# Windowed attention and a sine feed-forward on one core: crossbar transposes for batches 4 to 7, and a reordered start

## The chip, the cores and the metric

The kernel runs on one core of a Trainium2 chip. The metric is the device time in microseconds (us) of the whole program, the median of several runs. TensorE (PE in the profile) does matrix products, VectorE (DVE) and ScalarE (ACT) elementwise work, GpSimd (POOL) elementwise work and most loads, and SyncE (SP) issues copies and stores. In the profile's names KS and QS hold K and Q, VW the two layouts of V, VgX the rows of V of the global positions, and osb a tile of the output.

## The reference, cut to what matters

```python
# 8 batches, 8 heads, 576 positions, 64 per head; 8 global positions
scores = scale * q @ k^T
mask = |i - j| <= 32  or  i is global  or  j is global
attn = softmax(where(mask, scores, -1e9))
x = (attn @ v) as 4608 tokens x 512
h = x @ w_in                      # 512 x 2048
g = h + sin(alpha * h)**2 / (alpha + 1e-9)
out = g @ w_out                   # 2048 x 512
```

## The kernel before

The 4608 tokens are nine chunks of 512, and a batch is 576 tokens. Stage b (b = 1 to 7) is the attention of batch b, woven with the second matmul (`@ w_out`) of chunk b-1, and then the first matmul (`@ w_in`) of chunk b. A stage's length is measured here from the start of one first matmul to the start of the next (the first `hb<-xT` row of each chunk in the trace), so the length given for stage 1 holds the first matmul of chunk 0 and the attention of batch 1, and so on.

K and Q come in with positions on partitions, and TensorE transposes them for a pair of heads at a time. In stage b it transposes those of batch b+1:

```python
def T_half(src, b, hp, out):
    for jt in range(NTW):                       # 6 slices of 96 positions
        for t, pr in heads:
            nc.tensor.transpose(out=out[pr, jt*TW:(jt+1)*TW],
                in_=src[:, 2*hp + t, jt, :], identity=identb[0:TW, 0:TW])
# T_K, T_Q: T_half into PSUM, then one copy to kTw (VectorE) or qT (ScalarE)
```

V of a batch is used in two layouts. The second is made by SyncE with two DMAs inside SBUF once V has landed, and two more DMAs write the rows of the global positions:

```python
def shift_v(b, eng=nc.sync):
    eng.dma_start(out=W[0:64, 1], in_=W[QB:QB+64, 0])           # 384 KB
    eng.dma_start(out=W[64:KB, 1, :, 0:(NU-1)*D], in_=...)      # 240 KB
def global_v(b): ...                                             # 2 x 48 KB, SyncE
```

`gather_kq` loads the rows of K and Q of the global positions. The order of a stage's pieces is a list `parts` (one step of the attention each), into which the groups of the second matmul (`fill`, by `counts`) and loads are chained:

```python
counts = [1, 1, 1, 1, 1, 1, 2, 2, 4]
if p + 1 < B:
    with_extra(parts, load_slots(p + 1), 0, 4)   # K, Q in halves, then V: batch p+1
    if p < 3:
        parts[4] = partial(chain, parts[4], partial(gather_kq, p + 1))
    for hp in range(NHP):                        # global columns of K, Q (GpSimd)
        parts[hp + LEAD + 1] = partial(chain, ..., partial(globals_in, p + 1, hp))
...
if p == 0:
    m1[5] = partial(chain, m1[5], *vs)           # shift_v(1), global_v(1)
    m1[6] = partial(chain, m1[6], w_loads[3])    # second half of w_out
```

At the end of each attention, VectorE computes the 8 global columns (`xg`) and GpSimd inserts them into `xT` (8 copies). The first matmul waits for these insertions.

The softmax here doesn't subtract the row's maximum and nothing guards it: scores larger than these inputs give would overflow.

## Time and profile before

| | before |
|---|---|
| median of 3 runs | 361.02 us (360.83 to 362.65) |
| span of the profiled run | 356.8 us, granted clock 1.0 |
| PE busy | 336.7 us (94%) |
| stages 1 to 7, us | 40.19, 39.64, 36.94, 38.04, 36.71, 36.73, 34.42 |

The stage lengths are differences of starts in the instructions in order of time. The chain of work that ended last, by engine, from the page of before:

```profile
PE 65%; ACT 13%; DMA 7%; POOL 6%; issue 4%; DVE 3%; POOLq 1%; ACTq 0%; DVEq 0%
```

Two thirds of the chain is TensorE's own work (PEq, POOLq and the like are an engine's sequencer). SyncE's DMA issues in order of time (start, duration, queue, line, operation, out<-in, count), before:

```profile
37.85 0.57 SPq L143 DMA_DIRECT2D VW<-VW  x1
...
39.30 1.36 SPq L152 DMA_DIRECT2D VW<-VgX  x2
64.90 11.43 SPq L715 DMA_DIRECT2D out_dram<-osb  x4
```

The shifted copies of V of batch 1 are issued at 37.85, some 22 us before their first use at 60.21 and 27 us before SyncE's first output store.

### The profile page before, as it was taken

To read this page: it belongs to the slowest core of one execution; us is meant where nothing else is said; L and a number is where in the kernel's file an instruction comes from. 1 tells how busy PE (TensorE), PEld (TensorE's weight loads), DVE (VectorE), ACT (ScalarE), POOL (GpSimd) and SP (SyncE) were. 2 spreads that over 40 slices of the span, in tenths; PEclk is the share of its full clock that TensorE was granted. 3 is DMA by queue.
4 is the path that set the end of the run, shared out by engine and by line. 5 is a ranking of instruction groups with operands and counts; after the bars stand their busy time and mean duration, and the time that the engine had idled before them with its cause. 6 is when DMAs were issued, how large, how long until landed. Compare 5 with 4: busy or idle time off the path is not lost.

```text
span 356.8 us, 9407 instructions
## 1 busy us (share of the span) xinstructions
PE 336.7 (94%) x3738; PEld 172.0 (48%) x3738; DVE 237.4 (67%) x527; ACT 245.9 (69%) x376; POOL 205.6 (58%) x302
## 2 busy tenths in 40 slices
PE   6686997999999999999989999999999999999996
PEld 5563444444455445544554446444544444444444
DVE  5765784758775687668764878487848764875610
ACT  3756885847894889578975888488848884844401
POOL 9858897355871787169805791579247205755000
PEclk9999999999999999999999999999999999999999
DMA  9999999940598429940995099409931001001012
GB/s 75 166 196 184 199 170 179 182 136 20 35 171 104 112 17 168 122 114 3 165 115 134 2 121 154 136 8 90 181 105 43 30 32 61 0 2 59 31 59 88
DMA packets 133149, 35.39 MB, mean 99 GB/s; under 512 B 121794, under 2 KB 126818, under 8 KB 133106
## 3 DMA queue, kind: packets, MB, share of 16 engines
q0 software_dynamic: 123120, 20.04, 77.5%
q1 hardware_dynamic: 9682, 14.63, 13.9%
q8 instruction: 29, 0.48, 0.5%
q10 hardware_dynamic: 304, 0.14, 0.1%
q14 instruction: 14, 0.11, 0.1%
HBM read 38.95 MB, written 9.44 MB: 136 GB/s over the span
## 4 chain that ended last, share of the span: by engine, by line
PE 65%; ACT 13%; DMA 7%; POOL 6%; issue 4%; DVE 3%; POOLq 1%; ACTq 0%; DVEq 0%
PE hb L664 28%; PE o L703 12%; PE ops L703 12%; DMA w_out<-in_moe_w_out_dram 4%; ACT E L507 3%; PE num L553 3%; PE Sp L501 2%; DVE H2b L654 2%; ACT L607 2%; PE den L535 2%; DMA QS<-in_q_dram 2%; PE hb L703 2%; ACT Sb L671 2%; ACT lnd L541 2%; ACT L614 2%
## 5 line engine op out<-in xcount | busy, mean ns | idle before, releaser
L671 ACT ACTIVATE Sb<-hb,alphaT 128x512 bf16<-128x512 f32 x144 | 96.9, 684 | 57.6 <-PE hb L664 54.2
L664 PE MATMUL hb<-xT,w_in 128*128 128x512 bf16 x576 | 128.9, 379 | 1.6 <-POOL xT L588 1.4
L681 POOL TENSOR_TENSOR S<-Sb 128x512 bf16<-128x512 bf16 x94 | 96.0, 1041 | 48.2 <-ACT Sb L671 44.8
L654 DVE SCALAR_TENSOR_TENSOR H2b<-S,recipT,hb 128x512 bf16<-128x512 bf16 x144 | 102.4, 740 | 30.7 <-POOL S L681 30.3
L664 PEld LDWEIGHTS <-w_in 128*128 128x128 bf16 x576 | 55.7, 98 | 68.3 <-issue 1.8
L703 PEld LDWEIGHTS <-H2b 128*128 128x128 bf16 x560 | 49.6, 98 | 56.6 <-issue 2.5
L703 PE MATMUL ops<-w_out,H2b 128*128 128x512 bf16 x304 | 73.9, 380 | 1.5 <-DMA w_out<-in_moe_w_out_dram 1.5
L703 PE MATMUL o<-w_out,H2b 128*128 128x512 bf16 x224 | 54.4, 381 | 0.0
L588 POOL COPY xT<-xg 128x4 bf16 x64 | 12.9, 201 | 66.1 <-DVE xg L586 62.6
L507 ACT ACTIVATE E<-Sp 128x896 bf16<-128x896 f32 x48 | 43.5, 905 | 7.1 <-PE Sp L501 7.0
L572 DVE TENSOR_TENSOR xT<-num,rec 128x384 bf16<-128x384 f32 (+1 forms) x60 | 25.9, 453 | 23.1 <-PE num L553 18.3
L541 ACT ACTIVATE lnd<-den 128x384 f32<-128x384 f32 x48 | 23.7, 493 | 17.8 <-PE den L535 17.6
L513 DVE TENSOR_TENSOR E<-E,MASK 128x896 bf16<-128x896 bf16 x48 | 30.0, 626 | 6.4 <-ACT E L507 6.4
L553 PEld LDWEIGHTS <-VW 120*64 120x64 bf16 (+1 forms) x768 | 16.7, 114 | 20.0 <-issue 12.5
L543 ACT ACTIVATE rec<-lnd 128x384 f32<-128x384 f32 x48 | 25.1, 524 | 1.5
L501 PE MATMUL Sp<-qT,kTw 64*128 64x56 bf16 x768 | 19.7, 189 | 5.5 <-ACT qT L421 2.1
L465 DVE COPY kTw<-Kps 128x1344 bf16<-128x1344 bf16 x29 | 24.3, 839 | 0.0
L681 DVE TENSOR_TENSOR S<-Sb 128x512 bf16<-128x512 bf16 x34 | 17.6, 517 | 9.9 <-ACT Sb L671 9.8
L501 PEld LDWEIGHTS <-kTw 64*128 64x128 bf16 x768 | 15.4, 96 | 17.4 <-issue 11.5
L553 PE MATMUL num<-E,VW 120*64 120x56 bf16 (+1 forms) x720 | 20.3, 197 | 1.4 <-issue 1.2
L128 POOL DMA_DIRECT2D KS<-in_k_dram x18 | 20.7, 1152 | 0.6 <-issue 0.6
L128 POOL DMA_DIRECT2D QS<-in_q_dram x18 | 20.2, 1122 | 0.0
(133 smaller groups left out, 304.1 us busy)
## 6 DMA issues: line engine op xcount, KB each, us to landing
out_dram<-osb SPq DMA_DIRECT2D x35, 256.0 KB
KS<-in_k_dram POOLq DMA_DIRECT2D x14, 288.0 KB, 5.6
QS<-in_q_dram POOLq DMA_DIRECT2D x14, 288.0 KB, 10.2
VW<-in_v_dram POOLq DMA_DIRECT2D x12, 336.0 KB, 11.4
VW<-VW SPq DMA_DIRECT2D x7, 384.0 KB
w_in<-in_moe_w_in_dram POOLq DMA_DIRECT2D x2, 1024.0 KB, 15.3
w_out<-in_moe_w_out_dram POOLq DMA_DIRECT2D x2, 1024.0 KB, 16.0
VW<-VW SPq DMA_DIRECT2D x7, 240.0 KB
```

The source lines that it names most:

```text
L128: nc.gpsimd.dma_start(out=dst[:, h0 : h0 + nh].rearrange("p h t d -> p (h t) d"), in_=heads_ap(src, b, h0, 0, TW, 0, nh * NTW),)
L501: nc.tensor.matmul(out=Sp[:, t, m * QC : (m + 1) * QC], lhsT=kTw[hp][pr, i, :], rhs=qT[hp][pr, i, :], start=True, stop=True, skip_group_ch ...
L507: nc.scalar.activation(out=E[:], in_=Sp[:, :, 0:EW], func=AF.Exp, scale=scale)
L513: nc.vector.tensor_tensor(out=E[:], in0=E[:], in1=mk[:, None, :].to_broadcast([P, 2, EW]), op=ALU.mult)
L541: nc.scalar.activation(out=lnd[:], in_=den[:, :, 0:QB], func=AF.Ln)
L553: nc.tensor.matmul(out=num[pr, m, :], lhsT=W[0:nk, i % 2, 2 * hp + t, i // 2, :], rhs=E[0:nk, t, m * QC : (m + 1) * QC], start=b > 0 or m ...
L572: nc.vector.tensor_tensor(out=xT[:, hp, x0 : x0 + nb * QB].rearrange("p (u c) -> p u c", u=nb), in0=num[:, m0 : m0 + nb, 0:QB], in1=rec[:, ...
L654: nc.vector.scalar_tensor_tensor(out=H2b[:, n_, :], in0=s_[:], scalar=recipT[:, n_ : n_ + 1], in1=h_, op0=ALU.mult, op1=ALU.add,)
L664: nc.tensor.matmul(out=h2[:], lhsT=w_in[:, ci, nt * P : (nt + 1) * P], rhs=xT[:, ci, c * CH : (c + 1) * CH], start=(ci == 0), stop=(ci == ...
L671: nc.scalar.activation(out=Sb[:], in_=h2[:], func=AF.Sin, scale=alphaT[:, nt : nt + 1])
L681: eng.tensor_tensor(out=S2[:], in0=Sb[:], in1=Sb[:], op=ALU.mult)
L703: nc.tensor.matmul(out=ops[:], lhsT=H2b[:, nt, ts * P : (ts + 1) * P], rhs=w_out[:, nt, :], start=(nt == 0), stop=(nt == NT - 1),)
```

## The change

For batches 4 to 7 the transposes leave TensorE. GpSimd loads K and Q "raw", in 12 slices (96 positions, all heads), two stages ahead, SyncE transposes the slices by the DMA crossbar, and VectorE and ScalarE copy from SBUF. In stage 2 the loads change from halves to whole tensors. In the prologue (batch 0, before the first big matmul), scores 4 and 5 come sooner, ScalarE does half of the column insertions, and VectorE's reciprocal is moved. V of batch 1 is loaded after w_out instead of before it; hence its copies move from chunk 0's first matmul to the attention of batch 1. The core of the diff:

```diff
@@ new: raw loads, crossbar, copies
+    def x_loads(b):     # 12 loads of 96 KB: K slices, then Q slices
+    def cross(b, kq, jt):
+        nc.sync.dma_start_transpose(out=XT[kq][:, :, jt*TW:(jt+1)*TW], in_=src[:, jt]...)
+    def stage_X(b, hp): # VectorE copies to kTw, ScalarE to qT, now from SBUF
@@ column insertions of batch 0
-            nc.gpsimd.tensor_copy(
+            on_act = b == 0 and j >= NG // 2
+            copy, reg = (nc.scalar.copy, aregs[...]) if on_act else (nc.gpsimd.tensor_copy, pregs[j])
@@ prologue loads
-  pool_regs] + v_loads(1, ((0, H),)) + kq1[:2] + w_loads[2:3]
+  pool_regs] + kq1[:2] + w_loads[2:3]           # "kb" now also issues w_loads[3:]
@@ attention of stage p
-                    at = {2 + hp: [T_(p + 1, hp)] ...}
+                    at = {2 + hp: [partial(stage_X, p + 1, hp) if p > 2 else T_(p + 1, hp)] ...}
-                counts = [1, 1, 1, 1, 1, 1, 2, 2, 4]
+                counts = [2, 3, 3, 0, 1, 1, 0, 1, 3] if p == 1 else [1, 1, 1, 1, 1, 1, 2, 2, 4]
+                    if p == 1:
+                        parts[1] = partial(chain, parts[1], globals_v)
+                        parts[2] = partial(chain, *vs1, parts[2])     # shift_v(1), global_v(1)
+                        with_extra(parts, load_slots(2), 0, 4)
+                    else:
+                        ld = v_loads(p + 1, WHOLE)
+                        if p == 2:
+                            ld = [partial(gather_kq, 3)] + kq_loads(3, WHOLE) + ld
+                        xl = x_loads(p + 2) if p + 2 < B else []
+                        with_extra(parts, ld + xl[:NTW], 0, 4)
+                        with_extra(parts, xl[NTW:], 5 if p == 2 else 3, 3)
@@ first matmul of chunk p
-                    m1[5] = partial(chain, m1[5], *vs)
-                    m1[6] = partial(chain, m1[6], w_loads[3])
+                    m1[7] = partial(chain, m1[7], *v1)                # V of batch 1
+                    vs1 = vs
+                    if p > 1 and p + 2 < B:
+                        for i in range(2 * NTW):
+                            m1[1+i] = partial(chain, m1[1+i], partial(cross, p + 2, i // NTW, i % NTW))
```

(Cuts: the bodies of the new functions, the order string of the prologue, the reciprocal, one copy of Q moved to ScalarE there, the copies of the global columns of batch 1, and that in later chunks `shift_v` and `global_v` move from the eleventh piece of the first matmul to the first.)

## The prediction

> **What bounds the kernel now.** I read the page first (busy shares and the 40 slices), then the chain that ended last in order of time, which shows a repeating pattern, and then cut the span at that pattern's edges with the view of busy time by stretch. I call "stage b" the attention of batch b, woven with the second matmul of chunk b-1, followed by the first matmul of chunk b.
>
> ```profile
> PE 336.7 (94%) x3738; PEld 172.0 (48%) x3738; DVE 237.4 (67%) x527; ACT 245.9 (69%) x376; POOL 205.6 (58%) x302
> ...
> PE   6686997999999999999989999999999999999996
> ...
> DMA  9999999940598429940995099409931001001012
> ```
>
> TensorE is nearly full from the fourth slice on; the DMA engines are full for the first eight slices (some 71 us) and later only for part of each stage. So the steady part is a TensorE question and the start is a question of transfers.
>
> Busy time by stretch: us, then busy us (instructions) of PE, PEld, DVE, ACT, POOL, granted clock, DMA share, GB/s.
>
> ```profile
> 50.40:75.20 24.80, 22.52 (x342) 11.45 (x342) 15.19 (x39) 16.87 (x26) 14.62 (x26) 1.00 1.93 165
> ...
> 92.10:114.87 22.77, 22.50 (x365) 11.91 (x364) 15.74 (x39) 17.58 (x27) 14.75 (x27) 1.00 1.43 121
> ...
> 129.00:151.80 22.80, 22.53 (x365) 11.95 (x364) 15.98 (x40) 17.59 (x27) 13.42 (x25) 1.00 1.40 119
> 151.80:165.70 13.90, 13.90 (x67) 6.28 (x65) 10.64 (x16) 11.12 (x17) 9.80 (x10) 1.00 0.30 73
> 165.70:189.85 24.15, 22.71 (x365) 12.05 (x364) 15.91 (x40) 17.69 (x27) 13.33 (x25) 1.00 1.33 113
> ...
> 277.20:297.70 20.50, 20.25 (x269) 9.60 (x268) 12.91 (x36) 15.34 (x23) 3.06 (x10) 1.00 0.11 40
> ```
>
> The first row is the attention of stage 1, then stages 2, 3, the first matmul of stage 3, stage 4, and stage 7. Stage 7 is the natural experiment: it has no next batch to transpose, 96 TensorE instructions fewer (269 against 365), and takes 20.50 us against 22.80. The stretch of the first matmul (13.90 us) is TensorE alone.
>
> Two places at the start, from the instructions in order of time:
>
> ```profile
> 32.81 2.03 POOL L588 COPY xT<-xg 128x4 bf16 x8 [0.76 <-DVE xg L586]
> 34.88 5.34 PE L664 MATMUL hb<-xT,w_in 128*128 128x512 bf16 x24 [1.39 <-POOL xT L588]
> ...
> 59.26 1.02 PE L703 MATMUL ops<-w_out,H2b 128*128 128x512 bf16 x4 [1.49 <-DMA w_out<-in_moe_w_out_dram]
> ```
>
> The eight column insertions on GpSimd (2.03 us) are the last thing before the first big matmul, and stage 1 waits for the second half of w_out, issued at 43.25 and landed 16.0 us later.
>
> **What the Trainium skill says.** "DMA: Bandwidth & Descriptors", section "DMA Transpose (X-bar)": a plain DMA transpose is issued by Sync or Scalar, writes to SBUF and takes 2-byte types; the section "Issuing engines are not separate DMA queues" adds that all issuers share the same 16 engines. The trace of before agrees on the sharing (one DMA row, full while only GpSimd's loads and Sync's stores run); it has no transpose by DMA. "Advanced Engine Details and Errata", section "X-Bar Transpose (TRN2)": such transposes run about as fast as ordinary DMAs, 350-400 GB/s. No run yet shows it. "VectorE: DVE Perf Modes", section "Why PSUM operands drop a tier": a copy out of PSUM runs in a slower mode than one from SBUF. The trace has only the slow side: the copy of 1344 elements out of PSUM takes 839 ns.
>
> **The change part by part.**
>
> *Crossbar transposes, batches 4 to 7 (done in stages 3 to 6).* Removed per stage: 96 transposes, 4 pairs of heads x 24. The chain shows 12 of them at 0.26 us where they are back to back, so 8 x 0.26 = 2.1 us, and the last pair waits for the buffer that ScalarE empties after its table load (0.45 us again). Stage 7 says what that is worth in place: 22.80 - 20.50 = 2.30 us. What stays, unlike in stage 7: ScalarE's four qT copies (4 x 0.633 = 2.5 us, on an engine with 15.3 of 20.5 us taken) and VectorE's kTw copies, now three from SBUF, which I take as no dearer than 0.85. I give back 0.3 us for that. From the starts of the first matmuls in the chain, stages 3 to 6 take 36.94, 38.04, 36.72 and 36.72 us and stage 7 34.42; new stages at 34.42 + 0.4 = 34.8 save 2.1 + 3.2 + 1.9 + 1.9 = 9.1 us. Stage 4's extra 1.3 us is a TensorE gap of 1.17 us put down to "issue", which may come back elsewhere (a busier DMA), so I count 8.5 us.
>
> Added off the path: 12 loads in place of 4 on GpSimd. A load of 144 KB takes 0.88 us to issue and one of 288 KB 1.18, so one of 96 KB is some 0.8: 9.6 against 4.7 us, on an engine with about 13.4 of 22.8 us taken. It must be free for the column insertions at the stage's end; I expect that it is. Added on the transfer side: 12 transposes of 96 KB, 1.2 MB a batch. At the skill's rate that is 3.4 us of 16 engines (estimate); even at four times that it fits, because the DMA row is under half busy in a stage of 37 us and the results are not needed until the third unit of the next stage.
>
> *Stage 2 pays for it.* There the loads of batch 3 (still transposed by TensorE in that stage) are no longer four halves with the gather last, but the two gathers first, then K whole, then Q whole, and raw batch 4 behind. Before: first half of K issued at 93.52, landed 5.4 us later, at 98.9; TensorE wants the first pair of K at 102.47 and of Q at 102.72, just after they land. After: two gathers with their gaps 2 x (1.1 + 0.3) = 2.7 us later; a longer issue, 0.5; the second half of K, 1.8; all of Q, 3.6 (336 KB of V landed in 2.1 us, so 6.3 us per MB); one store of 256 KB in between, 0.8. Sum: 98.9 + 2.7 + 0.5 + 1.8 + 3.6 + 0.8 = 108.3. TensorE, in order, would stand 5.6 us at the first Q transposes. Of the 12.15 us that follow to the end of the stage at 114.87, some 10.3 are TensorE work, so about 1.8 is made good: cost 3.8 us.
>
> *w_out ahead of V of batch 1; stage 1.* The removed wait is 1.5 us, but V of batch 1 (4 to 5 us of transfer) and its shifted copy now land behind w_out, in a queue that is full anyway: V about 56, the shifted copy about 61. The second matmul's groups are pulled ahead ([2,3,3,0,...]) to cover that; the first V unit then runs at some 61.5 against 60.21, with five groups (4.4 us) fewer behind it, but ScalarE's units (lnd 0.49 + rec 0.53 + E 0.90) then bound the rest at about 12 us. End: 73.6 against 75.2. With the column insertion behind it I take 1.2 us.
>
> *Prologue.* Splitting the insertions saves some 1.0 us, scores 4 and 5 sooner 1 to 2 us (the second half of scores 4 waits for VectorE until 23.68, with the kTw copy held behind the VZ cast). But V of batch 1 lands when the queue lets it, and GpSimd now issues it in the first matmul of chunk 0 (2.6 us, with 8 insertions of 0.3), where it also squares: so most of this gain is waited away. I count nothing beyond the 1.2.
>
> Sum: 361.0 - 8.5 - 1.2 + 3.8 = 355.1.
>
> **The rivals.** (1) *No stall in stage 2*, because loads overlap better than my spacing says: 351. For it: the schedule looks tuned on a chip, and the fill of stage 1 is matched to a landing time. Against: the landing times add up. (2) *The crossbar takes the DMA engines.* If a transpose took 2 us of all 16 engines, 12 make 24 us beside some 15 of loads and stores and 4 of shifts: over the 35 us of a stage, each changed stage would become a transfer stage, and Sync's stores, queued behind the transposes, would stop osb: 370 or more. Against: the skill's rate; for: no run shows that rate for slices of 96 rows. (3) *GpSimd becomes the bound.* In GpSimd's instructions in order of time, the issue that came eighth after w_out waited for it to land, and the next one for the load after it:
>
> ```profile
> 59.49 1.05 POOL L259 DMA_INDIRECT GKQ<-in_k_dram,rowi  x1 [0.72 <-DMA w_out<-in_moe_w_out_dram]
> 61.60 1.42 POOL L259 DMA_INDIRECT GKQ<-in_q_dram,rowi  x1 [1.07 <-DMA KS<-in_k_dram]
> ```
>
> So I read a limit of eight loads in flight. With 14 to 18 loads a stage GpSimd blocks until the eighth before has landed; in stages 3 to 5 until some 14 us into the stage (harmless), in stage 2 until about 117, beside the stall. If the column insertions come after that, each stage loses 1 to 2 us: 357 to 360. (4) *The ScalarE bound*: four copies left in a shorter stage; if they sit on the path, stages save 1.5 instead of 2.1: 357.
>
> **Range and chances.** Between 355.1 (weight about two thirds) and 351 (one third) I put 354. The range 348.5 to 360 has the first rival with a better start below, rivals 3 and 4 above. The limit for faster by 2% is 353.8, in the middle: 0.47. Slower needs rival 2: 0.07. The rest, 0.46, is within 2%.
>
> **What would show it.** Stages 3 to 6 at some 34.8 us each, with 269 TensorE instructions in their attention; a wait of PE on the Q load in stage 2 of 4 to 6 us, at its first Q transposes; no PE wait on w_out in stage 1, its end 1 to 2 us sooner; 12 transposes done before the third unit of the next stage; GpSimd's insertions within 0.3 us of the vector result. Wrong would be: stage 2 no longer than 23 us (then 351 or less), PE waiting on column insertions or on osb in stages 3 to 6, or DMA full through the first matmuls.

## The result, and the profile after

| | before | after |
|---|---|---|
| median | 360.92 us (4 runs) | 376.10 us (4 runs, 374.94 to 379.08) |
| ratio | | 1.0429, 95% interval 1.0355 to 1.0502 |
| span of the profiled run | 356.8 us | 373.2 us |
| granted clock there | 1.0 | 0.941 |
| stages 1 to 7, us | 40.19, 39.64, 36.94, 38.04, 36.71, 36.73, 34.42 | 52.94, 48.50, 36.87, 35.58, 35.71, 34.74, 34.44 |

A ratio is the mean time of one kernel's runs over that of the other's of the same rounds, so not quite the ratio of the medians that are quoted. Executions over 1.5% slower than the fastest of the same kernel are left out of the means. The change is slower by 4.3%, and the time lies 16 us above the upper end of the predicted range.

The spans differ by 16.4 us, and the stages account for it: stage 1 +12.75, stage 2 +8.86, stages 3 to 6 together -5.52, and a start 0.25 later (35.13 against 34.88), which with stage 7 (+0.02) sums to 16.36. The page of after, in the rows of busy shares, clock and DMA by slice, and of the chain:

```profile
PE 335.0 (90%) x3354; PEld 165.1 (44%) x3354; DVE 234.8 (63%) x557; ACT 248.3 (67%) x381; POOL 217.7 (58%) x324
...
PE   4688988189994999989999999999999999999996
...
PEclk9557999579999699999999999999999999999999
DMA  9999999913019997899599959993914011000112
...
PE 43%; POOL 16%; DMA 16%; issue 10%; ACT 6%; DVE 5%; SPq 2%; POOLq 1%; ACTq 0%; DVEq 0%
```

There are 384 fewer TensorE instructions, as the change promised, but TensorE's share of the chain fell from 65% to 43%, and DMA and GpSimd took it over. The PE row has two holes (the slices with 1 and, later, 4), at about 65 to 75 us and 112 to 121 us. The clock row drops there or in the slice behind.

The holes themselves, in TensorE's instructions in order of time (start, duration, engine, line, operation, out<-in, count, and in brackets the wait and what ended it), in two windows of after:

```profile
61.84 1.89 PE L753 MATMUL ops<-w_out,H2b 128*128 128x512 bf16 x8
72.98 0.71 PE L598 MATMUL num<-E,VW 120*64 120x56 bf16 x16 [9.25 <-DMA VW<-VgX]
...
76.49 1.89 PE L753 MATMUL ops<-w_out,H2b 128*128 128x512 bf16 x4
...
85.09 2.76 PE L753 MATMUL o<-w_out,H2b 128*128 128x512 bf16 x12
```

```profile
118.06 0.45 PE L460 MATMUL Kps<-identb,KS 96*64 96x96 bf16 x12 [2.60 <-DMA KS<-in_k_dram]
...
122.18 0.69 PE L460 MATMUL qp<-identb,QS 96*64 96x96 bf16 x12 [3.68 <-DMA QS<-in_q_dram]
```

In stage 1 TensorE waits 9.25 us at the first value unit, for the last of the copies of V of batch 1. In stage 2 it waits 2.60 and 3.68 us for K and Q of batch 3. The row at 76.49 shows a second cost: four matmuls of 512 columns take 1.89 us, where elsewhere four take 1.04 and eight take 1.89. Busy time by stretch (columns as in the prediction; the column before the last two is the granted clock):

```profile
54.30:87.00 32.70, 21.92 (x313) 11.38 (x314) 13.51 (x36) 16.56 (x27) 12.73 (x21) 0.79 1.18 108
...
65.00:73.00 8.00, 0.02 (x2) 0.05 (x2) 0.00 (x0) 0.00 (x0) 0.47 (x3) 0.56 1.70 206
73.00:77.00 4.00, 3.73 (x70) 2.36 (x71) 2.52 (x9) 2.73 (x5) 0.48 (x2) 0.50 1.02 73
...
118.00:128.00 10.00, 6.26 (x90) 3.67 (x91) 2.86 (x6) 3.60 (x6) 5.66 (x9) 0.66 2.53 156
...
258.70:279.50 20.80, 20.53 (x270) 9.66 (x268) 14.93 (x49) 17.64 (x28) 8.16 (x20) 1.00 0.78 94
```

Cut finer, the granted clock is 0.50 from 65.94 us, 2.2 us after the last matmul ended (63.73), until 79.59, 6.6 us after work resumed; in stage 2 it is 0.50 from 120.55 to 127.38. The Trainium skill's "TensorE: Matmul & The Clock Gate", section "Part 1: The HAM clock gate", says that the array runs at half rate after an idle window of about 3.4 us and at full rate after a busy one. The two rates agree with this trace; the two delays measured here are not 3.4 us. The last row, stage 6, is what the change was meant to give: 20.80 us with 270 TensorE instructions.

Where did the 9.25 us come from? SyncE's issues in order of time, after:

```profile
61.22 0.38 SPq L765 DMA_DIRECT2D out_dram<-osb  x1
61.71 0.58 SPq L143 DMA_DIRECT2D VW<-VW  x1
...
63.15 1.37 SPq L152 DMA_DIRECT2D VW<-VgX  x2
```

and the DMA issues of the window 43 to 45 us (count, size, us from issue to landing):

```profile
VW<-in_v_dram POOLq DMA_DIRECT2D x1, 672.0 KB, 12.3
```

V of batch 1 was issued at 43.53 and landed 12.3 us later, at 55.8: the prediction's "about 56". But SyncE works in program order, its first output store stands ahead of the copies, and that store waits for the first output tile until 61.22. The copies follow at 61.71 and take until 72.9. So there are two suspects, the store ahead and the slow landing (GpSimd had issued 1.8 MB of batch 2's loads from 54.15 on).

In stages 3 to 5 GpSimd is late. Its instructions in order of time, stage 3 of after, followed by TensorE's first matmul:

```profile
154.86 4.61 POOL L490 DMA_DIRECT2D KS<-in_k_dram  x6
164.57 4.82 POOL L490 DMA_DIRECT2D QS<-in_q_dram  x6 [5.10 <-DMA VW<-in_v_dram]
...
171.35 2.04 POOL L636 COPY xT<-xg 128x4 bf16 x8
```

```profile
173.44 13.97 PE L714 MATMUL hb<-xT,w_in 128*128 128x512 bf16 x64 [0.85 <-POOL xT L636]
```

Two V loads and six raw K loads are under way; the ninth load, the first raw Q, stands 5.10 us until V has landed. That is the limit of eight loads in flight that the prediction read from before. In the packed trace GpSimd's loads take eight semaphores (107 to 114) in turn, and a load, with few exceptions, waits for the last use of its own: the limit lies in this program's waits, and no run shows whether the chip has one. The same load also waits for the last crossbar transpose of the batch before, which still reads the raw Q buffer. Of the two, V landed last, but not by much: 163.87 against 163.82 us here, 199.90 against 198.07 in stage 4 and 235.67 against 235.11 in stage 5. The insertions then start 0.96 us after their data (`xg` was ready at 170.39), and TensorE waits 0.85 us for them. The stage holds one more wait: the last Q transposes of batch 4 came late (issued at 156.38, landed at 163.82), ScalarE waited for them and TensorE, through the mask's product, for ScalarE:

```profile
164.05 0.67 ACT L693 COPY qT<-QS 128x576 bf16<-128x576 bf16 x1 [0.89 <-DMA QS<-QS]
...
166.44 0.38 PE L580 MATMUL den<-E,ones 120*64 120x448 bf16 x2 [0.96 <-DVE E L558]
```

### The profile page after: what moved, and what is told of

It is laid out like the page before. It is cut to its first block, busy times and chain, and to the rows that moved or that the text cites. A ratio compares the mean times of both kernels' runs of the same rounds, so it can differ in the third digit from the quotient of the medians.

```text
span 373.2 us, 8844 instructions
## 1 busy us (share of the span) xinstructions
PE 335.0 (90%) x3354; PEld 165.1 (44%) x3354; DVE 234.8 (63%) x557; ACT 248.3 (67%) x381; POOL 217.7 (58%) x324
## 3 DMA queue, kind: packets, MB, share of 16 engines
q1 hardware_dynamic: 29650, 19.35, 22.1%
## 4 chain that ended last, share of the span: by engine, by line
PE 43%; POOL 16%; DMA 16%; issue 10%; ACT 6%; DVE 5%; SPq 2%; POOLq 1%; ACTq 0%; DVEq 0%
PE hb L714 21%; PE ops L753 8%; DMA VW<-in_v_dram 6%; PE o L753 5%; DMA QS<-in_q_dram 5%; POOL S L731 4%; POOL QS L490 4%; DVE H2b L704 3%; DMA VW<-VgX 3%; DMA QS<-QS 2%; PE hb L753 2%; SPq L504 2%; POOL KS L128 2%; POOL xT L636 2%; ACT Sb L721 1%
## 5 line engine op out<-in xcount | busy, mean ns | idle before, releaser
L753 PE MATMUL ops<-w_out,H2b 128*128 128x512 bf16 x304 | 75.1, 384 | 0.0
L753 PE MATMUL o<-w_out,H2b 128*128 128x512 bf16 x224 | 55.3, 385 | 0.1
L636 POOL COPY xT<-xg 128x4 bf16 x60 | 12.3, 205 | 35.2 <-DVE xg L632 32.0
L598 PEld LDWEIGHTS <-VW 120*64 120x64 bf16 (+1 forms) x768 | 17.9, 119 | 30.1 <-issue 20.5
L598 PE MATMUL num<-E,VW 120*64 120x56 bf16 (+1 forms) x720 | 21.3, 201 | 10.0 <-DMA VW<-VgX 9.2
L490 POOL DMA_DIRECT2D QS<-in_q_dram x24 | 18.9, 797 | 15.8 <-DMA VW<-in_v_dram 15.8
L546 PEld LDWEIGHTS <-kTw 64*128 64x128 bf16 x768 | 16.2, 98 | 18.0 <-issue 12.1
L580 PE MATMUL den<-E,ones 120*64 120x448 bf16 x96 | 19.6, 404 | 2.3 <-DVE E L558 2.0
L490 POOL DMA_DIRECT2D KS<-in_k_dram x24 | 18.5, 787 | 3.4 <-DMA QS<-in_q_dram 1.8
```

The lines of the kernel that those rows point to most:

```text
L490: nc.gpsimd.dma_start(out=dst[:, jt], in_=bass.AP(tensor=src.tensor, offset=src.offset + (b * H * S + jt * TW) * D, ap=[[D, TW], [S * D, H ...
L546: nc.tensor.matmul(out=Sp[:, t, m * QC : (m + 1) * QC], lhsT=kTw[hp][pr, i, :], rhs=qT[hp][pr, i, :], start=True, stop=True, skip_group_ch ...
L598: nc.tensor.matmul(out=num[pr, m, :], lhsT=W[0:nk, i % 2, 2 * hp + t, i // 2, :], rhs=E[0:nk, t, m * QC : (m + 1) * QC], start=b > 0 or m ...
L753: nc.tensor.matmul(out=ops[:], lhsT=H2b[:, nt, ts * P : (ts + 1) * P], rhs=w_out[:, nt, :], start=(nt == 0), stop=(nt == NT - 1),)
```

## The experiments

Three theories stood at the start. **A:** stage 1 is long because V of batch 1 is no longer loaded first. **B:** stage 2 is long because GpSimd stands with eight loads in flight; its rival is the order of batch 3's K and Q loads, as the prediction had it. **C:** the half clock after the wait is itself a large part of stage 1. The stage lengths of all runs, from the profiled run of each:

| run | median us | ratio [95%] | stages 1 to 6, us |
|---|---|---|---|
| after | 376.10 | 1.0429 [1.0355, 1.0502] | 52.94, 48.50, 36.87, 35.58, 35.71, 34.74 |
| e1_v1_back | 364.59 | 1.0096 [1.0023, 1.0170] | 38.67, 49.52, 36.56, 36.33, 36.19, 34.72 |
| e2_halves | 378.15 | 1.0413 [1.0353, 1.0473] | 53.57, 47.34, 37.93, 36.84, 35.92, 34.85 |
| e3_both | 364.54 | 1.0069 [1.0015, 1.0124] | 40.16, 47.68, 36.72, 36.36, 35.92, 34.86 |
| e4_cross_only | 365.44 | 1.0069 [0.9984, 1.0154] | 39.93, 47.84, 37.68, 36.85, 35.59, 34.86 |
| e5_delay_b2 | 374.67 | 1.0374 [1.0327, 1.0421] | 52.73, 48.56, 37.10, 36.54, 36.68, 34.72 |
| e7_busy | 377.51 | 1.0491 [1.0453, 1.0530] | 52.95, 48.61, 39.01, 36.47, 36.84, 34.72 |
| e6_x_first | 360.83 | 1.0035 [1.0003, 1.0067] | 40.92, 47.55, 36.80, 34.84, 35.59, 34.75 |
| e9_raw_q_late | 357.44 | 0.9976 [0.9922, 1.0031] | 40.06, 41.65, 37.26, 36.80, 35.93, 34.86 |
| e5b_hold_b2 | 372.45 | 1.0370 [1.0323, 1.0416] | 48.93, 48.89, 36.91, 36.37, 35.36, 34.74 |
| e10_late_xfirst | 356.07 | 0.9904 [0.9874, 0.9935] | 43.12, 42.39, 37.28, 34.75, 35.93, 34.87 |
| e11_late_xfirst_pro | 355.75 | 0.9904 [0.9863, 0.9946] | 40.11, 41.74, 37.25, 34.76, 34.85, 34.90 |
| e13_shift_first | 370.68 | 1.0297 [1.0250, 1.0345] | 47.43, 48.42, 37.34, 35.99, 35.98, 34.73 |
| e14_shift_first_hold | 368.10 | 1.0212 [1.0172, 1.0252] | 45.34, 48.36, 35.95, 36.39, 36.35, 34.73 |
| e15_three_batches | 355.62 | 0.9872 [0.9841, 0.9903] | 39.17, 39.65, 36.94, 37.43, 34.74, 35.45 |

Ratios are to the kernel before on the same chip, whose medians were 359.2 to 361.9.

### Undoing parts of the change

**e1_v1_back** is the kernel after with V of batch 1 loaded first again, and its copies in the first matmul:

```diff
-  pool_regs] + kq1[:2] + w_loads[2:3]
+  pool_regs] + v1 + kq1[:2] + w_loads[2:3]
-  counts = [2, 3, 3, 0, 1, 1, 0, 1, 3] if p == 1 else [1, 1, 1, 1, 1, 1, 2, 2, 4]
+  counts = [1, 1, 1, 1, 1, 1, 2, 2, 4]
-  m1[7] = partial(chain, m1[7], *v1)
+  m1[5] = partial(chain, m1[5], *vs); m1[6] = partial(chain, m1[6], w_loads[3])
```

> The changed kernel with V of batch 1 loaded first again (its shifted and global copies in the first matmul of chunk 0, its column inserts, the fill counts and the w_out load where they were before). Theory A, that the 12.7 us which stage 1 lost come from V's copies landing behind w_out and behind the loads of batch 2: stage 1 back near 40 us (it was 52.9), no wait of PE on VW<-VgX, 362 to 365 us in all. Rival B, that the first stages lose to the half clock and to the prologue whatever the order: stage 1 stays over 46 us, total over 369.

Stage 1 falls from 52.94 to 38.67 us and the program by 11.5 us. The whole loss of stage 1 is in this part of the change (theory A). (The run also puts back the column insertions of batch 1 and, which its text does not say, the reciprocal. So do e3, e11 and e15: their "new prologue" lacks the moved reciprocal.)

**e2_halves** is the kernel after with batch 3's loads in halves again, and the gather behind them:

```diff
-  ld = [partial(gather_kq, 3)] + kq_loads(3, WHOLE) + ld
+  ld = load_slots(3); parts[4] = partial(chain, parts[4], partial(gather_kq, 3))
```

> The changed kernel with the loads of batch 3 in halves ahead of all else and the gather behind them, as before. Theory A, that stage 2 lost 8.9 us to K and Q landing late and to the slow clock after that wait: stage 2 near 40 us (it was 48.7), PE waits on KS and QS there gone, total 367 to 369. Rival B, that the doubled transfers of stage 2 (raw batch 4) delay K and Q in any order: stage 2 stays above 45 us, total over 372.

A miss for the order of loads; the rival had the numbers: stage 2 is 47.34 us, the program 378.15. TensorE no longer waits for K or Q, but the time is there under another name, as the next two runs show.

**e3_both** has both edits, and **e4_cross_only** also has the old prologue, so it is the kernel before with the crossbar alone.

> Both undone: what is left are the crossbar transposes and the new order of the prologue. If the losses add, 376 - 12.7 - 8.5 = 354 to 356 us, the first time that the change is faster than before; if stage 1 and stage 2 share a cause (the load queue as a whole), 358 or more.

> The kernel before with the crossbar transposes alone (stage 2's loads in halves). Stages 3 to 5 at 35 to 36.5 us, stage 6 at 34.7: 355 to 357. The difference to the run with both undone is the prologue's: theory A says under 0.7 us either way, as ScalarE's inserts wait for GpSimd's; the rival that scores sooner pay says that this one is 1 to 2 us slower.

Both miss what was expected (354 to 356 and 355 to 357 us). The ratio of both is 1.007: the crossbar with halves gains nothing, and whether it costs a little is open, as the interval of e4 takes in 1. The new prologue does not show (364.54 against 365.44 us, intervals overlap). Stage 2 of e4, TensorE and then GpSimd in order of time:

```profile
123.96 4.42 PE L708 MATMUL hb<-xT,w_in 128*128 128x512 bf16 x10 [7.87 <-POOL xT L632]
```

```profile
110.33 0.77 POOL L486 DMA_DIRECT2D KS<-in_k_dram  x1 [0.96 <-DMA VW<-in_v_dram]
113.21 1.02 POOL L259 DMA_INDIRECT GKQ<-in_k_dram,rowi  x1 [2.10 <-DMA VW<-in_v_dram]
...
121.81 2.09 POOL L632 COPY xT<-xg 128x4 bf16 x8
```

The 6.3 us of waits on K and Q have become one wait of 7.87 us on the column insertions. GpSimd stands at load after load, waiting for earlier ones to land, and reaches the insertions at 121.81 although their data was ready at 112.97. This supports theory B.

### Mending GpSimd's lateness

**e9_raw_q_late** is e4 with batch 4's six raw Q loads moved out of the attention into the first matmul, and the gather ahead of the raw loads:

```diff
-  with_extra(parts, xl[NTW:], 5 if p == 2 else 3, 3)
+  late = xl[NTW:] if p == 2 else []          # then: m1[i] = partial(chain, m1[i], late[i])
```

> The crossbar-only kernel with the six raw Q loads of batch 4 moved out of the attention of stage 2 into the first matmul behind it, and the gather of batch 3 ahead of raw K. Theory E, that stage 2 loses 8 us because GpSimd, blocked by loads in flight, comes 7.9 us late to the column inserts: the PE wait on xT falls from 7.9 to under 1 us, stage 2 from 47.8 to 40 to 42 us, total 356 to 358, the first faster than before. Rival B, that the doubled transfers cost that time wherever they are issued: the wait moves into the first matmul (squares) or stage 3, total over 361.

Stage 2 falls from 47.84 to 41.65 us. Theory B is shown for this stage: with fewer loads ahead of the insertions the wait on them shrinks, though not to the "under 1 us" expected. For the whole program the interval of the ratio takes in 1.

```profile
116.60 3.61 PE L708 MATMUL hb<-xT,w_in 128*128 128x512 bf16 x16 [1.85 <-POOL xT L632]
```

**e6_x_first** is e4 with V issued between raw K and raw Q in stages 3 to 5, so that the ninth load comes later:

```diff
-  with_extra(parts, ld + xl[:NTW], 0, 4); with_extra(parts, xl[NTW:], 3, 3)     # p > 2
+  with_extra(parts, xl[:NTW] + ld + xl[NTW:], 0, 4)                              # p > 2
```

> The crossbar-only kernel, with V of the next batch issued between the six raw K loads and the six raw Q loads in stages 3 to 5, and not ahead of both. Theory D, that at most eight loads are in flight and the seventh raw load waits for V (4 to 5 us of GpSimd a stage), which holds back the column inserts: GpSimd's waits on VW there go from 4 to 5 us each to under 1, PE's waits on inserts in stages 3 to 5 (0.8 to 0.9 each) go, 1.5 to 3 us less than that kernel. Rival: another wait ends the stage, same time.

Stage 4 falls from 36.85 to 34.84 us; stage 5 stays at 35.59, and the ratio falls only from 1.0069 to 1.0035, with intervals that overlap. In both stages GpSimd meets the other wait, which the totals of GpSimd's waits in e6 name (us in total, times, longest): the raw Q buffer is still being read by the last crossbar transposes of the batch before. In stage 4 (3.2 us) the insertions still come in time, in stage 5 (4.1 us) TensorE waits 0.84 us for them.

```profile
POOL QS L486 <- DMA QS<-QS: 7.4, 2, 4.1
```

**e10_late_xfirst** has both mends, with the old prologue, and **e11_late_xfirst_pro** the same with the new prologue.

> The kernel before with the crossbar alone, the raw Q loads of batch 4 moved to the first matmul of stage 2, and in stages 3 to 5 the values loaded between raw K and raw Q: both repairs of GpSimd's blocking together. Theory (what ate the crossbar's gain is GpSimd standing in the queue of loads in flight, so that its column insertions come late): stage 2 is about 41 us as with the first repair alone, stages 3 to 6 are 34.8 to 36.8 us, no wait of PE on a column insertion over 1 us in stages 4 and 6, total 354 to 357, ratio 0.985 to 0.997. Rival (the crossbar itself costs the time, through DMA engines or ScalarE): the repairs do not add, stages 3 to 5 stay at 36 to 37.5 us, total 357 to 361.

> The same kernel with the change's new prologue (scores 4 and 5 sooner, half of the column insertions on ScalarE, the two-engine reciprocal). Theory (the new prologue gives nothing because ScalarE's insertions wait for GpSimd's on the same tile and the keep-warm matmuls run at half rate): the first matmul starts within 0.5 us of the run without it, total within 1 us of it. Rival (the new prologue is worth 1 us or more where nothing else spoils stage 1): first matmul 1 us or more sooner, total 1 us or more shorter.

The mends add up: ratio 0.9904 for both, 1% faster than before. So most of what ate the crossbar's gain was GpSimd's lateness and not the crossbar. The expectation for stage 2 (about 41 us) is met loosely (42.39 and 41.74), as is "34.8 to 36.8" for stages 3 to 6, since stage 3 is 37.28 and 37.25. The price of e9's edit stands there: with six raw Q loads among its squares GpSimd keeps VectorE and TensorE waiting, and the first matmul of the stage takes 16.33 us in e11, against 14.10 in before. The attention behind it takes 20.92 us, as in stage 6 of after (20.93). In e11, from all engines' instructions in order of time:

```profile
125.06 1.58 POOL L490 DMA_DIRECT2D QS<-in_q_dram  x2
...
128.54 4.04 PE L712 MATMUL hb<-xT,w_in 128*128 128x512 bf16 x16 [0.69 <-DVE H2b L702]
```

In e10 a wait of 0.84 us on the insertions remains in stage 5. Its stage 1 (43.12) also had waits on w_out of 2.3 us and a clock of 0.83 between 60 and 70 us, in this one profiled run (358.98 us, the slowest of its six). The new prologue starts the first big matmul 0.96 us sooner in the profile (34.23 against 35.19), between theory and rival, but the medians differ by 0.32 us, and in e3 it starts 1.37 us later than in e4 (37.56 against 36.19): a gain is not shown.

### Taking stage 1 apart

**e5_delay_b2** is the kernel after with batch 2's loads later in the program:

```diff
-  with_extra(parts, load_slots(2), 0, 4)
+  with_extra(parts, load_slots(2), 3, 4)
```

> The changed kernel, but in stage 1 the loads of batch 2 are issued three units later, behind the first V unit's place. Theory A1, that V's shifted and global copies of batch 1 (issued at 61.7 to 64.5, landed at 72.9) crawl because batch 2's loads fill the same 16 DMA engines: they land 3 to 4 us after issue, PE waits on VW<-VgX 2 to 3 us in place of 9.2, stage 1 near 46 us in place of 52.9, total 369 to 371. Rival A2, that V itself lands late or that the small copy is slow by itself: the wait stays over 7 us.

Inconclusive: GpSimd is far ahead of TensorE and nothing holds it, so it still issued the loads at 53.0 to 60.8 us. The wait stayed at 9.1 us. A place in the program is no time.

**e7_busy** is the kernel after with 44 extra matmuls (results unused) while TensorE waits, to keep the clock up:

```diff
+  def busy(): ...                 # 44 matmuls of 448 columns into a spare PSUM tile
+  parts[3] = partial(chain, busy, parts[3])
```

> The changed kernel with 44 matmuls of 448 columns on the side (results unread) in the place where PE waits in stage 1, some 8.2 us of work. Theory C, that the wait costs twice, once as idle time and once as matmuls at half speed for about 6 us after it: the matmuls after it run at full rate (four of 512 columns in 1.0 us, not 1.9), stage 1 1.5 to 2.5 us shorter, total 374. Rival: the slow matmuls there are hidden behind ScalarE or V's copies and the time stays at 376.

TensorE's wait fell to 1.23 us, the first value unit ran at 72.88, much as in after (72.98), and stage 1 stayed at 52.95. From the first value unit to the next first matmul it took 14.84 us, against 15.09 in after. But this is no test of theory C: the clock fell to 0.50 all the same, only later, from 75.39 to 78.80, just over the next matmuls of 512 columns:

```profile
76.61 1.49 PE L754 MATMUL ops<-w_out,H2b 128*128 128x512 bf16 x3 [0.33 <-issue]
```

What a full clock is worth shows in e14 below.

**e5b_hold_b2** repeats e5 with a real hold: a small GpSimd copy that reads the result of batch 1's first value unit stands ahead of batch 2's loads.

```diff
+  hold = partial(nc.gpsimd.tensor_copy, out=xhold[:], in_=xT[:, 0, S:S+1])
+  parts[3] = partial(chain, parts[3], hold)
-  with_extra(parts, load_slots(2), 0, 4)
+  with_extra(parts, load_slots(2), 3, 4)
```

> The kernel after, with one thing moved: the loads of batch 2 stay behind a small GpSimd copy that reads the output of batch 1's first value unit, so none of them can be under way while the values of batch 1 and their copies move. Theory A1 (the copies of batch 1's values take 9.7 us because batch 2's loads share the DMA engines with them): the larger copy lands 3 to 5 us after its issue, PE waits at most 3 us at the first value unit, stage 1 (start of first matmul to start of the next) falls from 52.9 to 45 to 48 us; stage 2 may pay for the later loads (1 to 4 us longer), total 366 to 373. Rival A2 (the values were simply issued too late, or the copy of 48 KB pieces is slow by itself): the copy still takes 8 us or more, PE waits over 7 us, stage 1 stays over 51 us.

TensorE's wait falls from 9.25 to 4.16 us and stage 1 to 48.93, neither quite A1's "at most 3" and "45 to 48" nor A2's "over 7" and "over 51". Taking the sharing of the DMA engines away takes 5.1 us off the wait. The stretch from 58 to 61.5 us gave away the rest (e5b, busy time by stretch):

```profile
58.00:61.50 3.50, 3.44 (x52) 1.94 (x53) 1.01 (x3) 3.44 (x6) 0.00 (x0) 1.00 0.00 0
```

The last two columns are DMA share and GB/s: nothing moves. V has landed, yet the copies are not issued until 62.13, right behind the output store at 61.64.

**e13_shift_first** is the kernel after with the copies one step earlier in SyncE's program, ahead of the store:

```diff
-  parts[1] = partial(chain, parts[1], globals_v)
-  parts[2] = partial(chain, *vs1, parts[2])
+  parts[1] = partial(chain, globals_v, *vs1, parts[1])
```

> The kernel after, with the two shifted copies and the global copies of batch 1's values put ahead of the first output store in SyncE's program (one step of the attention earlier); nothing else. Theory (the copies' lateness has three terms: the values land late, SyncE stands at an output store before it issues the copies, and batch 2's loads share the engines): SyncE issues the first copy when the values have landed, at 59 to 60.5 us instead of 61.7, and PE's wait at the first value unit falls by 1 to 2.5 us from 9.2; stage 1 is 50 to 52 us, total 372 to 375. Rival (the store is what matters): PE's wait falls below 5 us, stage 1 below 48 us.

My theory missed and its rival was right on both numbers (wait below 5 us, stage 1 below 48). SyncE, and TensorE's first value unit, in e13:

```profile
55.55 0.57 SPq L143 DMA_DIRECT2D VW<-VW  x1
...
60.50 22.46 SPq L765 DMA_DIRECT2D out_dram<-osb  x4
```

```profile
67.22 0.70 PE L598 MATMUL num<-E,VW 120*64 120x56 bf16 x16 [3.65 <-DMA VW<-VgX]
```

The copies go out at 55.55 instead of 61.71, when V lands. One line of program order is worth 5.5 us of stage 1.

**e14_shift_first_hold** has both, the order and the hold.

> The same with batch 2's loads held behind the first value unit of batch 1 as well, which alone brought PE's wait from 9.2 to 4.2 us and stage 1 from 52.9 to 48.9. Theory (three terms that add): the values have landed by 56 us, SyncE issues the copies then, they land at 60.5 to 62 us, before PE asks for them at about 64; PE's wait at the first value unit is below 0.5 us, the clock stays at 1.0 there, and stage 1 falls to 41.5 to 44.5 us; stage 2 may be longer by 0 to 3 us, total 363 to 369. Rival (the late issue of the values by itself spoils stage 1, by the order of the second matmul's groups): stage 1 stays above 46 us though the wait is gone.

```profile
64.99 0.44 PE L599 MATMUL num<-E,VW 120*64 120x56 bf16 x16
...
75.25 2.76 PE L754 MATMUL o<-w_out,H2b 128*128 128x512 bf16 x12
80.61 2.75 PE L715 MATMUL hb<-xT,w_in 128*128 128x512 bf16 x12 [2.60 <-POOL xT L637]
```

The wait is gone, and the clock is 1.00 in every stretch of 5 us from 50 to 80 us. So this run, and not e7, bears on theory C. From the first value unit to the last group of the second matmul TensorE has the same instructions in e14 and in after: 10.26 us (64.99 to 75.25) at full clock, and 12.11 us (72.98 to 85.09) in after, with 6.6 us at half rate. The half clock behind the wait is thus worth 1.85 us of the 12.75, one profiled run against another; in e7, with 3.4 us at half rate, the stretch took 11.87 us. Theory C is right in that size and small beside the wait.

Stage 1 is 45.34, a little over the 41.5 to 44.5 expected, because the hold has a cost of its own that I had not counted: GpSimd gets to the column insertions late, and TensorE waits 2.60 us. Without that it would be 42.7 (45.34 - 2.60, an estimate). The remaining difference to before lies in the first matmul, which took 18.15 us to the first `w_out` group (35.27 to 53.42) against 15.58 (34.88 to 50.46); 1.28 us of it is a wait of the transposes there for VectorE's copy, which before does not have, and the clock stood at 0.50 until 37.78. What follows, without the 2.60 us, is 24.59 us against 24.61. Stage 2 is 48.36, as in after: it is not a consequence of stage 1.

### A version that beats both

**e15_three_batches** is e11 with batch 4 transposed by TensorE again:

```diff
-  partial(stage_X, p + 1, hp) if p > 2 else T_(p + 1, hp)
+  partial(stage_X, p + 1, hp) if p > 3 else T_(p + 1, hp)
-  xl = x_loads(p + 2) if p + 2 < B else []
+  xl = x_loads(p + 2) if 2 < p < B - 2 else []
```

> The kernel with both repairs of GpSimd's blocking and the new prologue (355.75 us, ratio 0.990), but batch 4 transposed by TensorE again, as before; the crossbar serves batches 5 to 7 alone. Theory (batch 4's crossbar gains nothing, since its raw loads crowd stage 2 and GpSimd is late there and in stage 3): stage 2 is 39.4 to 40 us again and stage 3 about 37 to 38, stages 4 to 6 34.8 to 36, total 352.5 to 356, ratio 0.979 to 0.990. Rival (the crowding only moves on by one stage): stage 3 is 39 us or more, total 356 to 359, no better than with four batches.

Stage 2 is 39.65 us, as in before, so the raw loads of batch 4 were the reason for its last 2 us. Stage 3 is 36.94 and stage 4 is 37.43, with 16.36 us in its first matmul, so some crowding moves on, but less than it saves. At 355.62 us and a ratio of 0.9872 this is 1.3% faster than before. Against e11 (0.9904, on another chip) the intervals overlap, so that the three-batch version is better than the four-batch one is not shown by these runs.

## Why the prediction was wrong

**Stage 1, "I take 1.2 us" of gain: 12.75 us of loss.** The step that failed is "V about 56, the shifted copy about 61". The first half was right (55.8). The second took for granted that SyncE would issue the copies when V landed, and that they would move in a few us. SyncE stood at an output store until 61.22 (e13 without it: wait 3.65 us in place of 9.25), and batch 2's loads shared the DMA engines with the copies (e5b without them: 4.16 us). Together they make the whole wait (e14: none). In the landing of the copy that TensorE waits for the two add: 72.84 us in after, 67.08 in e13 (5.8 sooner), 68.17 in e5b (4.7) and 62.34 in e14 (10.5), there 2.65 us before TensorE asks for it. The prediction read GpSimd's queue in detail and never asked for SyncE's order, although its view of before shows the copies 27 us ahead of the first store. The half clock is a consequence of the wait and added 1.85 us (e14 against after). Of the sharing of the DMA engines, which the prediction took from the skill, the DMA row of before is no evidence, as it is a mean over all queues; e5b is.

**Stage 2, "cost 3.8 us": 8.86 us.** The mechanism was right: TensorE stood at the first Q transposes and, with the K ones, for 6.28 us against the 5.6 predicted. The term that was mis-sized is "about 1.8 is made good". Nothing was, and the stage lost 2.58 us beside the waits: the clock was 0.50 until 127.38, so the first 5.2 us of work after the wait ran at half rate, some 2.6 us lost (an estimate). And the cause goes deeper than the load order. With the order repaired (e2, e3, e4) the same time came back as a wait of 7.5 to 7.9 us on column insertions, because GpSimd, held at eight loads in flight, was late. The prediction named this as a rival ("in stage 2 until about 117, beside the stall") but took it as parallel to the stall, not as the next bound. Moving six loads, and the gather ahead of the rest (e9), brings back 6.2 of the 8.2 us that e4 loses in this stage, at the price of some 2.2 us in the next one's first matmul.

**Stages 3 to 6, "34.8 us each, 8.5 us saved": 36.87, 35.58, 35.71, 34.74; 5.52 us saved.** Stage 6, which has no raw loads of its own, is as predicted, with 270 instructions for the 269 predicted. So the reading of stage 7 as a natural experiment was right. VectorE's three copies from SBUF were as cheap as taken: 447, 237 and 176 ns (medians), against 839 for the one from PSUM; an element of the large one took 0.40 ns against 0.62. In stages 3 to 5 the words "(harmless)" failed: the ninth load waits 4 to 5 us, and the insertions come 1 us late, which costs TensorE 0.85 us in each. Stage 3 also lost 0.96 us to the late Q transposes, so its attention took 22.77 us where stage 6 took 20.93. Stage 4 of e6, e10 and e11, at 34.75 to 34.84, shows the predicted length with that wait taken away.

**Prologue, nothing beyond the 1.2: right in the number, for another reason.** The prediction let the gain be waited away behind the first matmul. In after, the vector result came 1.16 us sooner (31.39 against 32.55), yet the first matmul started 0.25 us later. ScalarE's insertions waited for GpSimd's on the same tile, and the seven keep-warm matmuls, almost the last thing before the first matmul, ran at half rate (3.10 us for what took 1.67 before). The clock there differs from run to run with one and the same prologue (with the old one it was full from 27.37 us in before, and 0.50 until 33.30 in e9), so this part may be chance:

```profile
31.73 3.10 PE L834 MATMUL ops<-VW,identb 112*128 112x512 bf16 x7 [1.77 <-DVE alphaT L380]
...
32.68 0.93 ACT L636 COPY xT<-xg 128x4 bf16 x4 [1.65 <-POOL xT L636]
```

**Rivals.** The crossbar as the bound of every stage (rival 2) fell, with stage 6; what remained of it is the 0.96 us of stage 3. GpSimd as a bound (rival 3) was right in kind but put at 357 to 360, since each stage was given 1 to 2 us; in stage 2 it costs 8. ScalarE as a bound (rival 4) did not show in stage 6. The chance of "slower" was 0.07 because only rival 2 led there; that two transfers could go wrong in order, on an engine without any work to be seen, was not among the rivals, so "slower" came true by a path that the prediction had not weighed.

**Left open:** what share of stage 2's 8.86 us the load order alone would cost without the raw loads (no run has whole loads and late raw loads), and how much of the wait at the ninth raw load each of its two holders, V and the raw Q buffer, would make alone (e6 takes away only the first).

## What to carry to other kernels

When a load moves, follow everything that hangs on it through every issuing engine: a copy is issued when its data has landed and when its engine's program has come to it, so look at what stands ahead of it in that engine's order. An engine that both loads and does the last step of a stage must not be filled with loads ahead of that step; when removing a wait gives no time, look for the same microseconds under the next name. A filler that only moves a slow stretch is no test of what that stretch costs: check in the trace that the state is gone. A saving in TensorE instructions is worth its time only where loads and helpers still finish ahead of TensorE, so apply it stage by stage and leave out the stage that pays for it.

## What the Trainium skill lacked or had wrong

- "DMA: Bandwidth & Descriptors", section "Issuing engines are not separate DMA queues", calls the time to initiate a DMA usually small relative to the DMA. Here each crossbar transpose of 96 KB took SyncE 1.2 us (median 1207 ns), of 2.3 us from the start of its issue to its landing where nothing else moved, and twelve took 15.5 us of its program (from 176.86 to 192.40 in after). The section gives no issue time for a transpose; the page has one only in a table about another generation of the chip, in a column for "previous generations".
- "Advanced Engine Details and Errata", section "X-Bar Transpose (TRN2)", gives 350 to 400 GB/s. The runs don't show that rate. From 185 to 189 us of after only transposes move: the DMA engines are busy for 0.39 of the time at 79 GB/s, 203 GB/s if they were busy throughout (an estimate). Over the whole program the hardware queue's packets took 13.9% of 356.8 us before and 22.1% of 373.2 us after, so 32.9 us of all engines more for 4.72 MB more, or 143 GB/s, among other transfers.
- No page read here tells a reader to look for the wait at the ninth load, which decided stage 2 in e2 to e4 and had a part in stages 3 to 5 (5.10 and 4.12 us in stages 3 and 4 of after). The traces show it as the program's own, with eight semaphores in turn; they don't show a limit of the chip.
- "TensorE: Matmul & The Clock Gate", section "Part 1: The HAM clock gate", agrees in the rates, 1.00 and 0.50, but not in the delays of about 3.4 us: in after, e13 and e5b the clock fell 2.2, 2.6 and 2.3 us after the last matmul ended and came back 6.6, 5.8 and 8.4 us after work resumed. In stage 1 of after this cost 1.85 us (against e14).
